# Turning a pair's attention probabilities with one wide transpose, and summing values in quarters of 32 rows

## The chip, the core and the metric

The kernel runs on one core of one Trainium2 chip. The metric is the device time of one execution in microseconds; the median of three runs of the kernel before is 863.86 (863.07 to 864.49). TensorE is called PE in the profile (PEld for its weight loads), VectorE is DVE, ScalarE ACT, GpSimd POOL, and the queue that issues most DMAs is SP.

## What is computed

Attention over 8 batches of 8 heads, 576 tokens, 64 dimensions, followed by a feed-forward layer over the joined heads:

```python
mask_local = (rel >= 0) & (rel < stride)                                  # stride 32
mask_strided = (rel >= 0) & (pos[None, :] % stride == pos[:, None] % stride)
masks = [mask_local if h < H // 2 else mask_strided for h in range(H)]
scores = where(masks, scale * (q @ k.T), -1e9)
attn = softmax(scores)                       # max subtracted, sum + 1e-9
x = (attn @ v) -> 4608 tokens x 512
h = x @ w_in                                 # 512 x 2048
g = maximum(h, 0) + log1p(exp(-abs(h)))
out = g @ w_out                              # 2048 x 512
```

## The kernel before

**Pairs of heads.** Two heads are worked on together: a pair n of 32 in all, four to a batch. The first eight (batches 1 and 2) run in an opening part whose order is written out by hand. The other 24, n = 8 to 31, are the ones that the change touches. In strided heads the tokens are sorted by their class beforehand, so that in both kinds of head a block of 32 queries sees only 64 keys: its own block and the one before it. There are 18 blocks to a head. They are held as nine blocks in each of two halves of the partitions ("place" 0 and 1), and in each half 32 partitions are for one head and 32 for the other.

**Stages of one pair.** `head_scores` (L402) makes 36 matmuls of 64 rows of weights by 32 columns, with 64 columns of keys streamed: nine blocks, two places, two heads. Six blocks of a place go to the bank ps, three to the upper part of the bank po; in those three the two heads change places in the partitions (`place_of`), and their matmuls are interleaved with the other ones. `add_mask` (L461) adds the mask on DVE in two pieces and brings the scores to SBUF. Row maximum, subtraction, exponential (ACT), row sum and normalisation follow, on tiles of 128x576. Then `prob_transposes` (L516) turns the probabilities in blocks of 32 by 32: per pair 16 DVE instructions, which write a layout of tiles with 96 queries and 128 keys. `weighted` (L584) makes 12 matmuls over it: six tiles of queries, two heads, with 128 rows, of which 32 keys overlap with the next tile, and 96 columns streamed. The first six go to the lower part of the next pair's bank po, the others to a bank ph. `x_part` copies each half to the input of the feed-forward layer, first its high part on ACT (L635), then the remainder by a subtraction on DVE (L633).

**The feed-forward layer.** It works on chunks of 512 tokens. `hidden` (L718) makes 12 matmuls into a bank ph for 128 of the 2048 hidden features; ACT (L730 to L735) and DVE (L742) make the softplus, ACT and DVE split it into a high and a low part (L287, L772), and `output` (L787) makes 12 matmuls into the four banks py. Later chunks go in pairs by products of sums (L890). There are two ph banks.

**The order.** From batch 3 on a planner (`Plan`) sets it: each task has a due time, an engine, a cost and tasks that it follows, and the tasks are issued in the order of planned starts. Between two pairs stand three steps of the feed-forward layer. On PE the scores of pair n and the weighted sums of pair n-1 form one task; with it 22 pairs' scores stand together with another pair's sums, two blocks of scores stand alone, and two blocks of sums. Behind such a block stands one `output`, then a `hidden`. For it the planner asks that the subtractions of the pair's sums be done, and its ph bank must have been read by L742.

**Loads.** `load_v` fetches a pair's values with two DMAs on SP (96 rows, then 128 rows by five tiles) into `v_in`; it is issued once the pair before has been summed. The masks come once in the beginning, as bf16, on ACT's queue.

Of the kernel before, what the change touches and what calls it, by code (L numbers as in the profile page):

```python
# [9 lines left out]
F32 = mybir.dt.float32  # L10
F32R = mybir.dt.float32r
BF16 = mybir.dt.bfloat16
# [6 lines left out]
P = 128  # L19
# [5 lines left out]
SPLIT = [(0, 6), (6, 9)]  # L25
# [51 lines left out]
class Plan:  # L77
# [8 lines left out]
    def add(self, name, urgency, engine, cost, fn, after=(), late=0.0):  # L86
        self.tasks[name] = (urgency, len(self.tasks), engine, cost, fn, after, late)
# [29 lines left out]
def attention_softplus_ffn(  # L117
# [75 lines left out]
    def x_at(part, k, c):  # L193
# [13 lines left out]
        early[part, PAIRS[-1]][:, lo : lo + 4 * TILE].rearrange("p (h a c) -> p h a c", h=2, a=2)  # L207
        for part, lo in (("l", PAD + S), ("l", PAD + S + 4 * TILE), ("h", 2 * S))
    ]
    qT = homes[0][:, 2 * S : 3 * S]  # L210
    kT = [homes[2][:, i * (PAD + S) : (i + 1) * (PAD + S)] for i in range(2)]
    v_in = homes[1][:, 2 * S : 2 * S + 2 * NTILE * D]
    prob_all = homes[1][:, : 2 * S]
    prob = [t.rearrange("p (a c) -> p a c", c=64) for t in (prob_all[:, :S], prob_all[:, S:])]

# [39 lines left out]
    def k_of(n):  # L255
        return kT_early[n] if n < NPAIR else kT[n % 2]
# [11 lines left out]
    def prob_of(n):  # L268
        if n < NPAIR:
            chunks = prob_early[n][:, PAD:].rearrange("p (a c) -> p a c", c=3 * PAD)  # L270
            return chunks[:, :, :64]
        return prob[n % 2]
# [37 lines left out]

    def load_v(n):
        b, pair = order[n]
        if n < NPAIR:

            t = room[n]
        else:
            t = v_in
        t = t[:, : 2 * NTILE * D].rearrange("p (a c) -> p a c", c=2 * D)
        src = v[b, pair]
        nc.sync.dma_start(t[PAD:P, 0], src[0:TILE])  # L320
        src = src[TILE - PAD : 2 * TILE]
        src = bass.AP(
            tensor=src.tensor,
            offset=src.offset,
            ap=[src.ap[0], [TILE * 2 * D, NTILE - 1], src.ap[1]],
        )
        nc.sync.dma_start(t[:, 1:NTILE], src)
        vs[n] = t.rearrange("p a (h d) -> p a h d", d=D)
# [12 lines left out]
    def mask_of(n, part):  # L341

        if is_local(n):
            return mask_b[:, : 6 * 64] if part == 0 else mask_b[:, 64 : 4 * 64]
        if part == 0:
            return mask_b[:, 6 * 64 : 9 * 64].unsqueeze(1).broadcast_to([P, 2, 3 * 64])
        return mask_b[:, 9 * 64 :]
# [38 lines left out]
    def head_scores(n):  # L386

        taken.append(n)
        pss[n, 0] = ps_s.tile([P, 512], F32, tag="ps", name=f"ps_{n}")
        shared[n] = ps_o.tile([P, 512], F32, tag="po", name=f"po_{n}")  # L390
        pss[n, 1] = shared[n][:, S // 2 :]
        for x in range(6):
            for chunk in (x, x + 3) if x > 2 else (x,):
                part = chunk // 6
                for place in range(2):
                    a, i = block_at(chunk, place)
                    c = TILE * a + 32 * i
                    for h in range(2):
                        to = 64 * place + 32 * place_of(part, h)
                        head = slice(64 * h, 64 * h + 64)  # L400
                        at = 64 * (chunk - SPLIT[part][0])
                        nc.tensor.matmul(  # L402
                            pss[n, part][to : to + 32, at : at + 64],
                            lhsT=qT[head, c : c + 32],
                            rhs=k_of(n)[head, c : c + 64],
                            start=True,
                            stop=True,
                        )
# [98 lines left out]
    def prob_transposes(n, quarters=range(4)):  # L507
        p = prob_of(n)
        for quarter in quarters:
            for place, h in (divmod(quarter, 2),):  # L510
                for part, (lo, hi) in enumerate(SPLIT):
                    row = 64 * place + 32 * place_of(part, h)
                    src = p[row : row + 32]
                    a, i = block_at(lo, place)
                    for c in range(2):
                        nc.vector.transpose(  # L516
                            pt[
                                32 * (i + c) : 32 * (i + c) + 32,
                                h,
                                a : a + hi - lo,  # L520
                                32 * i : 32 * i + 32,
                            ],
                            src[:, lo:hi, 32 * c : 32 * c + 32],
                        )

    def early_transposes(n, g):
# [602 lines left out]
    plan = Plan()  # L1129
    add = plan.add  # L1130

    def lows_of(c):
        return [
            f"L{n}{half}"
            for n in range(2 * NPAIR, len(order))
            if START[c] < (order[n][0] + 1) * S and START[c] + CH[c] > order[n][0] * S
            for half in range(2)
        ]
# [49 lines left out]
            add(f"G{c}.{f}", when[old] + 2.5, "SP", 0.8, fn, after, 3.5)  # L1188

    def sums_of(n):  # L1190
        for half in range(2):
            weighted(n, half, n not in alone)

    def scores_of(n, x, y, name, e, cost, after, also=None):

        z = x - 11.0
        if n > 2 * NPAIR:
            add(f"Q{n}", z, "ACT", 1.4, lambda n=n: lay_out_q(n), [f"q{n}", f"S{n-1}"])

        def work():  # L1200
            head_scores(n)
            if also is not None:
                sums_of(also)

        add(name, x, e, cost, work, after)
        for j in range(2):
            fn = lambda j=j: add_mask(n, j)
            add(f"Y{n}{j}", y + j, "DVE", 0.47, fn, [f"S{n}", f"P{n-2}"])
        after = [f"Y{n}0", f"Y{n}1"]
        for j, (letter, e, cost, fn) in enumerate(  # L1210
            (
                ("x", "DVE", 0.75, row_maxima),
                ("s", "DVE", 0.75, row_subtract),
                ("E", "ACT", 0.7, row_exp),
                ("z", "DVE", 0.75, row_sums),
                ("g", "DVE", 0.16, lambda n: guard(n, nc.vector)),
                ("R", "DVE", 0.2, reciprocals),
                ("M", "DVE", 0.75, lambda n: normalize(n, nc.vector)),
            )
        ):  # L1220
            add(f"{letter}{n}", y + 1.5 + j, e, cost, lambda fn=fn: fn(n), after)
            after = [f"{letter}{n}"]
        for j in range(4):
            name = f"P{n}" if j == 3 else f"P{n}.{j}"
            fn = lambda j=j: prob_transposes(n, (j,))
            add(name, y + 8.5 + 1.3 * j, "DVE", 1.25, fn, after)
            after = [name]
        if n + 2 < len(order):
            add(f"k{n+2}", x + 5, "SP", 0.8, lambda: load_k(n + 2), [f"S{n}"], 2.0)
            add(f"q{n+2}", x + 18, "SP", 0.8, lambda: load_q(n + 2), [f"P{n}"], 2.0)  # L1230
# [432 lines left out]
```

## Time and profile before

| | us |
|---|---|
| median of three runs | 863.86 |
| the profiled execution | 865.16 |
| its span, first to last instruction | 863.1 |
| DVE busy on L516, 448 transposes | 140.7 |
| sum of the records of PE multiplies on L402, by bank (2016 records) | 27.8 and 22.0 |
| ACT busy in all | 492.2 |

A row of the page's fifth part names line, engine, operation, tiles and shape, then the summed time and the mean of one instruction. PE's records overlap, so their summed times are not the time that PE spends: that is read from when the next block starts. In the instructions in order of time, neighbours with the same line and tiles are merged, with their count at the end. The idle time in brackets is that of the engine before the row, with what ended it.

### The profile page before, as it was taken

Reading aid. Unit: us, or ns where it says so; the run is one execution under the profiler, and the core shown is the slowest. Engines: PE = TensorE matmul, PEld = TensorE weight load, DVE = VectorE, ACT = ScalarE, POOL = GpSimd, SP = SyncE. Lnnn points to the kernel's source line nnn. Section 1 sums busy time; section 2 is a strip of 40 time slices with the busy share of each in tenths; the row PEclk is TensorE's granted clock in tenths of the full one; section 3 lists DMA queues with packets and bytes.
Section 4 is the critical chain, followed back from the end, with each engine's and each line's share of the span. In section 5 each row is a group of like instructions: output and inputs, shape, how many; then the busy total and the mean of one; then the engine's idle time right before and its main releaser. Section 6 shows DMA issues by size and latency. Waiting matters only on the chain.

```text
span 863.1 us, 16559 instructions
## 1 busy us (share of the span) xinstructions
PE 853.4 (99%) x6536; PEld 700.7 (81%) x6536; DVE 640.9 (74%) x1370; ACT 492.2 (57%) x913; POOL 65.9 (8%) x88
## 2 busy tenths in 40 slices
PE   7999999999999999999999999999999999999998
PEld 6787888888888888888888888888888888888886
DVE  7899977898798879888788976677687746656500
ACT  6898755655555555546555555766664355566400
POOL 6345550000000000000000000000000000000000
PEclk9999999999999999999999999999999999999999
DMA  9794114646313453135424433655546143333100
GB/s 330 284 348 155 55 42 152 205 148 218 119 46 99 132 185 106 58 107 164 126 86 145 142 106 118 202 176 169 175 147 197 50 158 134 111 124 120 47 27 24
DMA packets 74477, 119.49 MB, mean 138 GB/s; under 512 B 5664, under 2 KB 41632, under 8 KB 74400
## 3 DMA queue, kind: packets, MB, share of 16 engines
q1 hardware_dynamic: 74112, 118.12, 41.4%
q8 instruction: 51, 0.84, 0.4%
q10 hardware_dynamic: 288, 0.33, 0.1%
q14 instruction: 26, 0.21, 0.1%
HBM read 88.01 MB, written 30.41 MB: 137 GB/s over the span
## 4 chain that ended last, share of the span: by engine, by line
PE 92%; DVE 4%; ACT 2%; issue 1%; DMA 0%; POOL 0%; ACTq 0%; POOLq 0%
PE py L787 43%; PE ph L718 23%; PE bank_a L890 10%; PE bank_c L890 5%; PE bank_b L890 2%; PE pv L584 2%; PE ps L402 2%; PE po L584 2%; PE py_last L787 1%; PE po L402 1%; PE pt L554 1%; DVE home L516 1%; DVE a_i L672 0%; DVE a_o L672 0%; DMA raw_q<-in_qk_dram 0%
## 5 line engine op out<-in xcount | busy, mean ns | idle before, releaser
L787 PE MATMUL py<-w_o,gh 128*128 128x512 f32 x1024 | 318.5, 392 | 0.0
L787 PEld LDWEIGHTS py<-w_o,gh 128*128 128x128 f32 x1024 | 190.3, 188 | 41.4 <-DVE o L287 0.3
L718 PE MATMUL ph<-x_h,w_i 128*128 128x512 f32 x656 | 202.8, 390 | 0.5 <-DVE u L742 0.5
L787 PE MATMUL py<-w_o,gl 128*128 128x512 f32 x512 | 199.3, 389 | 0.0
L516 DVE STREAM_TRANSPOSE home<-home 32x192 f32<-32x192 f32 x448 | 140.7, 318 | 7.1
L718 PEld LDWEIGHTS ph<-x_h,w_i 128*128 128x128 f32 x656 | 122.6, 188 | 26.7 <-POOL home L505 0.9
L718 PE MATMUL ph<-x_l,w_i 128*128 128x512 f32 x328 | 127.7, 389 | 0.0
L287 ACT CAST gh<-u 128x512 fp32r<-128x512 f32 x89 | 55.2, 621 | 107.7 <-DVE u L742 84.7
L787 PEld LDWEIGHTS py<-w_o,gl 128*128 128x128 f32 x512 | 96.1, 188 | 20.3
L730 ACT ACTIVATE u<-ph 128x512 f32<-128x512 f32 x84 | 50.1, 598 | 90.8 <-PE ph L718 88.2
L772 DVE TENSOR_TENSOR gl<-u,gh 128x512 fp32r<-128x512 f32 x117 | 80.8, 691 | 19.3 <-ACT gh L287 15.7
L735 ACT ACTIVATE u<-u 128x512 f32<-128x512 f32 x144 | 90.9, 632 | 3.8
L733 ACT ACTIVATE u<-u 128x512 f32<-128x512 f32 x144 | 90.9, 632 | 3.6
L718 PEld LDWEIGHTS ph<-x_l,w_i 128*128 128x128 f32 x328 | 61.6, 188 | 13.0
L742 DVE SCALAR_TENSOR_TENSOR u<-ph,u 128x512 f32<-128x512 f32 x84 | 57.7, 687 | 13.7 <-ACT u L735 12.5
L730 ACT ACTIVATE u<-kept 128x512 f32<-128x512 f32 x45 | 28.4, 631 | 41.1 <-DVE kept L986 25.6
L287 DVE COPY o<-py 128x512 f32<-128x512 f32 (+1 forms) x15 | 10.0, 669 | 45.6 <-PE py L787 45.5
L986 DVE TENSOR_TENSOR kept<-bank_c,kept 128x512 f32<-128x512 f32 x15 | 10.4, 692 | 33.8 <-PE bank_c L890 33.8
L287 ACT COPY home<-home 128x576 f32<-128x576 f32 x26 | 33.4, 1284 | 1.7 <-DMA home<-in_qk_dram 1.7
L287 ACT COPY o<-py 128x512 f32<-128x512 f32 (+1 forms) x21 | 11.5, 574 | 38.4 <-PE py L787 27.6
L461 DVE TENSOR_TENSOR home<-ps,home 128x384 f32<-128x384 f32 x28 | 15.5, 554 | 23.5 <-PE ps L402 22.0
L981 ACT COPY kept<-bank_a 128x512 f32<-128x512 f32 x30 | 17.6, 586 | 25.8 <-PE bank_a L890 24.2
(197 smaller groups left out, 1188.7 us busy)
## 6 DMA issues: line engine op xcount, KB each, us to landing
home<-in_qk_dram SPq DMA_DIRECT2D x56, 288.0 KB, 3.2
ws<-far SPq DMA_DIRECT2D x30, 512.0 KB, 3.3
home<-in_v_dram SPq DMA_DIRECT2D x28, 320.0 KB, 3.8
out_dram<-o SPq DMA_DIRECT2D x35, 256.0 KB, 2.4
ri<-in_moe_w_in_dram SPq DMA_DIRECT2D x16, 512.0 KB, 7.4
ro<-in_moe_w_out_dram SPq DMA_DIRECT2D x16, 512.0 KB, 8.3
far_w<-w_i SPq DMA_DIRECT2D x16, 512.0 KB, 4.7
w_i<-far_w SPq DMA_DIRECT2D x16, 512.0 KB, 3.3
```

What stands on the lines that cost most here:

```text
L287: (engine.copy if engine is nc.scalar else engine.tensor_copy)(dst, src)
L402: nc.tensor.matmul(pss[n, part][to : to + 32, at : at + 64], lhsT=qT[head, c : c + 32], rhs=k_of(n)[head, c : c + 64], start=True, stop=True,)
L516: nc.vector.transpose(pt[32 * (i + c) : 32 * (i + c) + 32, h, a : a + hi - lo, 32 * i : 32 * i + 32,], src[:, lo:hi, 32 * c : 32 * c + 32],)
L584: nc.tensor.matmul(po[64 * h : 64 * h + 64, TILE * x : TILE * x + TILE], lhsT=vs[n][:, a, h, :], rhs=pt_of(n, a)[:, h, a % 2], start=True, ...
L718: nc.tensor.matmul(ph, lhsT=w_i(c, f)[:, half, cc * P : (cc + 1) * P], rhs=x_at(x, cc, c), start=(i == 0), stop=(i == 3 * NCC - 1),)
L730: nc.scalar.activation(us[c, f], phs[c, f], AF.Abs)
L733: nc.scalar.activation(u, u, AF.Exp, scale=-1.0)
L735: nc.scalar.activation(u, u, AF.Ln, bias=1.0)
L742: nc.vector.scalar_tensor_tensor(to, in0=ph, scalar=0.0, in1=u, op0=ALU.max, op1=ALU.add)
L772: engine.tensor_tensor(g, us.pop((c, f)), ghs[c, f].bitcast(F32), op=ALU.subtract)
L787: nc.tensor.matmul(y_of(c, t), lhsT=g[:, sl], rhs=w32["o", f][:, half], start=(f == ROWS[c][0] and n == 0), stop=(f == ROWS[c][-1] and n = ...
L890: nc.tensor.matmul(bank, lhsT=w_left(p, A, f, half, i), rhs=x_right(p, A, part, i), start=p in "125" and n == 0, stop=n == 5, skip_group_c ...
```

## The change

For pairs 8 to 31, and for these alone:

- Scores: the nine blocks of a place are now nine neighbouring blocks of the sequence, in order, and the heads keep their 32 partitions in all of them. The count and the shapes of the matmuls stay.
- One transpose of 128x576 (`turn`) takes the place of the 16. It writes `turned`: for each quarter of 32 partitions (place and head) and each block, 32 keys by 32 queries, twice (the block before and the own one).
- `turned_sums` takes the place of `weighted`: for each of nine blocks, two key blocks, two places and two heads a matmul with 32 rows of values (64 columns of weights) and 32 queries streamed, two of them accumulated: 72 matmuls instead of 12. Place 0 goes to the bank that took the first half before, place 1 to that of the second, and the two are filled side by side.
- `load_v` fetches the values so that each quarter has its head's blocks of 32 keys: four DMAs in pieces of 64 elements instead of two.
- A mask in the new order of blocks is loaded once more for the strided heads, in six DMAs.
- In the planner the four tasks of the transposes become one with a cost of 0.8.

```diff
+    turned = homes[0][:, :S].rearrange("p (x c l) -> p x c l", c=2, l=32)
+    v_turned = homes[1][:, 2 * S : 2 * S + (NCHK + 1) * D]
+    mask_turned = homes[0][:, 3 * S : 3 * S + NCHK * 32].bitcast(BF16)
...
     def load_v(n):
         b, pair = order[n]
+        if n >= 2 * NPAIR:
+            t = vs[n] = v_turned.rearrange("p (x d) -> p x d", d=D)
+            if n == 2 * NPAIR:
+                nc.gpsimd.memset(t[:64, 0], 0.0)
+            for place in range(2):
+                blocks = slice(32 * (NCHK * place - place), 32 * NCHK * (place + 1))
+                src = v[b, pair][blocks].rearrange("(x k) (h d) -> h k x d", k=32, h=2)
+                for h in range(2):
+                    at = 64 * place + 32 * h
+                    nc.sync.dma_start(t[at : at + 32, 1 - place :], src[h])
+            return
...
     def head_scores(n):
...
+        if n >= 2 * NPAIR:
+            for chunk in range(NCHK):
+                part = chunk // 6
+                at = 64 * (chunk - SPLIT[part][0])
+                for place in range(2):
+                    c = 32 * (NCHK * place + chunk)
+                    for h in range(2):
+                        to = 64 * place + 32 * h
+                        head = slice(64 * h, 64 * h + 64)
+                        nc.tensor.matmul(
+                            pss[n, part][to : to + 32, at : at + 64],
+                            lhsT=qT[head, c : c + 32],
+                            rhs=k_of(n)[head, c : c + 64],
...
+            return
...
+    def turn(n):
+        src = prob_of(n).rearrange("p x (c l) -> p x c l", l=32)
+        nc.vector.transpose(
+            turned.rearrange("p x c l -> p (x c) l"), src.rearrange("p x c l -> p (x c) l")
+        )
+
+    def turned_sums(n, joint):
...
+        pos[n, 0], pos[n, 1] = banks_
+        for x in range(NCHK):
+            for c in range(2):
+                for place in range(2):
+                    for h in range(2):
+                        at = 64 * place + 32 * h
+                        rows = slice(at, at + 32)
+                        nc.tensor.matmul(
+                            banks_[place][64 * h : 64 * h + 64, 32 * x : 32 * x + 32],
+                            lhsT=vs[n][rows, x + c],
+                            rhs=turned[rows, x, c],
+                            start=c == 0,
+                            stop=c == 1,
                         )
...
     def sums_of(n):
-        for half in range(2):
-            weighted(n, half, n not in alone)
+        turned_sums(n, n not in alone)
...
-        for j in range(4):
-            name = f"P{n}" if j == 3 else f"P{n}.{j}"
-            fn = lambda j=j: prob_transposes(n, (j,))
-            add(name, y + 8.5 + 1.3 * j, "DVE", 1.25, fn, after)
-            after = [name]
+        add(f"P{n}", y + 8.5, "DVE", 0.8, lambda: turn(n), after)
```

On PE, the block of a pair's scores and of the sums of the pair before, in the middle of the program, before (ps and po take the scores, po and pv the sums, home_94 to home_96 are the SBUF rooms of queries and probabilities, of values, and of keys):

```order
L718 MATMUL ph_13_3614<-x_l_594,w_i_13_3558 128x512
L402 MATMUL ps_3638<-home_96,home_94 32x64 x16
L402 MATMUL po_3639<-home_96,home_94 32x64 x4
L402 MATMUL ps_3638<-home_96,home_94 32x64 x4
L402 MATMUL po_3639<-home_96,home_94 32x64 x4
L402 MATMUL ps_3638<-home_96,home_94 32x64 x4
L402 MATMUL po_3639<-home_96,home_94 32x64 x4
L584 MATMUL po_3639<-home_94,home_95 64x96 x6
L584 MATMUL pv_3682<-home_94,home_95 64x96 x6
L787 MATMUL py_106<-w_o_1590,gh_11_3585 128x512 x2
```

and the same block with the change, where the two rows of sums repeat 18 times:

```order
L417 MATMUL ps_4017<-home_96,home_94 32x64 x24
L417 MATMUL po_4018<-home_96,home_94 32x64 x12
L583 MATMUL po_4018<-home_94,home_95 64x32 x2
L583 MATMUL pv_1_4055<-home_94,home_95 64x32 x2
L583 MATMUL po_4018<-home_94,home_95 64x32 x2
```

The two banks of scores no longer alternate, and those of sums do; apart from these blocks PE's order is the same in both programs.

On DVE behind such a block, before (L461 adds the mask, L633 makes the low part of the sums, L742 the softplus, L516 turns):

```order
L461 TENSOR_TENSOR home_95<-ps_3638,home_97 128x384 [waits DMAHW0_49,PE_49]
L461 TENSOR_TENSOR home_95<-po_3639,home_97 128x192 [waits PE_49,Activation_49]
L633 TENSOR_TENSOR x_l_406<-po_3639,x_h_364 128x256
L633 TENSOR_TENSOR x_far_3714<-po_3639,x_far_3714 128x32
L466 TENSOR_REDUCE st_3716<-home_95 128x9 [waits DVE_49]
L633 TENSOR_TENSOR x_far_3714<-pv_3682,x_far_3714 128x288 [waits Activation_49]
L742 SCALAR_TENSOR_TENSOR u_13_3689<-ph_13_3614,u_13_3689 128x512
...
L505 TENSOR_TENSOR home_95<-home_95,st_3716 128x576 [waits DVE_49]
L516 STREAM_TRANSPOSE home_94<-home_95 32x6x32 [waits DVE_49]
L516 STREAM_TRANSPOSE home_94<-home_95 32x6x32
L516 STREAM_TRANSPOSE home_94<-home_95 32x3x32 x2
```

and with the change:

```order
L494 TENSOR_TENSOR home_95<-ps_4017,home_94 128x384 [waits DMAHW6_49,PE_49]
L494 TENSOR_TENSOR home_95<-po_4018,home_94 128x192 [waits PE_49,Activation_49]
L698 TENSOR_TENSOR x_l_406<-po_4018,x_h_364 128x256
L698 TENSOR_TENSOR x_far_4147<-po_4018,x_far_4147 128x32
L499 TENSOR_REDUCE st_4149<-home_95 128x9 [waits DVE_49]
L698 TENSOR_TENSOR x_far_4147<-pv_1_4055,x_far_4147 128x288 [waits Activation_49]
L807 SCALAR_TENSOR_TENSOR u_13_4128<-ph_13_4000,u_13_4128 128x512
...
L538 TENSOR_TENSOR home_95<-home_95,st_4149 128x576 [waits DVE_49]
L562 STREAM_TRANSPOSE home_94<-home_95 128x576 [waits DVE_49]
L807 SCALAR_TENSOR_TENSOR u_14_4197<-ph_14_4164,u_14_4197 128x512 [waits Activation_49]
```

The lines are numbered anew, and the order up to the softplus stands as before, with the second mask piece still waiting for ACT; the transposes are one instruction.

More of the change, by code (lines that the diff above doesn't have):

```diff
@@ L344, in mask_of @@
             return mask_b[:, : 6 * 64] if part == 0 else mask_b[:, 64 : 4 * 64]
+        if n >= 2 * NPAIR:
+            return mask_turned[:, : 6 * 64] if part == 0 else mask_turned[:, 6 * 64 :]
         if part == 0:
@@ L391, in head_scores @@
         pss[n, 1] = shared[n][:, S // 2 :]
+        if n >= 2 * NPAIR:
+            for chunk in range(NCHK):
[10 more added lines that the diff above has]
+                            rhs=k_of(n)[head, c : c + 64],
+                            start=True,
+                            stop=True,
+                        )
+            return
         for x in range(6):
@@ L523, in prob_transposes @@
                             src[:, lo:hi, 32 * c : 32 * c + 32],
+                        )
+    def turn(n):
+        src = prob_of(n).rearrange("p x (c l) -> p x c l", l=32)
+        nc.vector.transpose(
+            turned.rearrange("p x c l -> p (x c) l"), src.rearrange("p x c l -> p (x c) l")
+        )
+    def turned_sums(n, joint):
+        if joint:
+            banks_ = [shared[n + 1], ps_h.tile([P, 512], F32, tag="ph", name=f"pv_{n}_1")]
+        else:
+            taken.append(n)
+            banks_ = [
+                ps_o.tile([P, 512], F32, tag="po", name=f"pv_{n}_0"),
+                ps_s.tile([P, 512], F32, tag="ps", name=f"pv_{n}_1"),
+            ]
+        pos[n, 0], pos[n, 1] = banks_
[11 more added lines that the diff above has]
+                            stop=c == 1,
                         )
@@ L1130, in attention_softplus_ffn, with load_mask @@
     add = plan.add
+    def load_mask():
+        for place in range(2):
+            to = mask_turned[64 * place : 64 * place + 64].rearrange("p (a x c) -> p x a c", x=3, c=64)
+            for x, (half, at) in enumerate(((0, 6), (place, 9), (1, 6))):
+                src = masks[64 * half : 64 * half + 64, 64 * at : 64 * at + 3 * 64]
+                nc.sync.dma_start(to[:, x], src.rearrange("p (a c) -> p a c", c=64))
+    add("mask", 0.0, "SP", 1.5, load_mask, [], 2.0)
     def lows_of(c):
```

## Prediction

> **What bounds the kernel now.** I read the page's busy rows first, then the table of stages, then the instructions in order of time around one pair of heads.
>
> ```profile
> span 863.1 us, 16559 instructions
> PE 853.4 (99%) x6536; PEld 700.7 (81%) x6536; DVE 640.9 (74%) x1370; ACT 492.2 (57%) x913; POOL 65.9 (8%) x88
> PE 92%; DVE 4%; ACT 2%; issue 1%; DMA 0%; POOL 0%; ACTq 0%; POOLq 0%
> 134.00:500.00 366.00, 366.00 (x3309) 300.96 (x3302) 309.63 (x721) 207.02 (x358) 0.00 (x0) 1.00 0.41 132
> 548.00:700.00 152.00, 152.00 (x1001) 125.35 (x988) 108.98 (x217) 84.40 (x144) 0.00 (x0) 1.00 0.48 151
> ```
>
> The last two rows are stages in microseconds, with the busy time of PE, PEld, DVE, ACT and POOL. They hold nearly all the work that changes, and in both PE has no idle time at a granted clock of 1.00. DVE has 56 us spare in the first and 43 us in the second. So the time moves by what PE's instructions cost, and by any wait put in front of them; work taken from DVE buys nothing there. This is one pair's block on PE, with what ACT and DVE do behind it:
>
> ```profile
> 188.39 0.39 PE L718 MATMUL ph<-x_l,w_i 128*128 128x512 f32 x1
> 188.71 0.48 PE L402 MATMUL ps<-home,home 64*32 64x64 f32 x20
> 188.98 0.24 PE L402 MATMUL po<-home,home 64*32 64x64 f32 x1
> 189.01 0.24 PE L402 MATMUL ps<-home,home 64*32 64x64 f32 x4
> 189.04 0.26 PE L402 MATMUL po<-home,home 64*32 64x64 f32 x3
> ...
> 189.50 0.27 PE L402 MATMUL po<-home,home 64*32 64x64 f32 x4
> 189.70 0.72 PE L584 MATMUL po<-home,home 128*64 128x96 f32 x12
> 190.24 0.67 PE L584 MATMUL pv<-home,home 128*64 128x96 f32 x12
> 190.64 0.38 ACT L635 CAST x_h<-po 128x288 fp32r<-128x288 f32 x1
> 190.84 0.73 PE L787 MATMUL py<-w_o,gh 128*128 128x512 f32 x2
> ...
> 191.06 0.36 DVE L461 TENSOR_TENSOR home<-po,home 128x192 f32<-128x192 f32 x1 [0.76 <-ACT x_h L635]
> ...
> 192.78 0.68 DVE L742 SCALAR_TENSOR_TENSOR u<-ph,u 128x512 f32<-128x512 f32 x1
> ...
> 193.69 0.62 PE L718 MATMUL ph<-x_h,w_i 128*128 128x512 f32 x2
> ```
>
> Columns: start, length, engine, line, operation, output and inputs, rows*columns of the weights, shape, count. An f32 matmul leaves two records, so 36 score matmuls (L402) are 72 records and 12 weighted sums (L584) are 24. Scores take 189.70 - 188.71 = 0.99 us from first start to the next block's; the sums take 190.84 - 189.70 = **1.14 us**. Sums run at two records per 82 ns (the last of 24 starts at 190.24 + 0.67 - 0.25 = 190.66, and the first round takes some 50 ns more); the switch to the next block takes 190.84 - 190.66 = 0.18 us.
>
> **The change, part by part.** *Weighted sums.* Twelve matmuls of 128 rows by 96 columns become 72 of 32 rows by 32 columns: 144 records for 24, in four quarters of the array, 36 each. No such record is in the trace, so I bound a round, that is one record in each quarter. The multiply alone: the scores' 64 columns take 56 ns a round (next fence), 96 columns take 82, so 32 take about 30. But every record first loads its own 64 columns of weights:
>
> ```profile
> L402 PEld LDWEIGHTS ps<-home,home x1344: 102/107/108, 33.0 to 644.0; 64*32 64x32 f32 x192
> L584 PEld LDWEIGHTS pv<-home,home x372: 132/137/138, 60.8 to 671.0; 128*64 128x64 f32 x186
> L787 PEld LDWEIGHTS py<-w_o,gh 128*128 128x128 f32 x1024 | 190.3, 188 | 41.4 <-DVE o L287 0.3
> 11.96 0.91 PE L372 MATMUL py<-early_l,early_h 128*64 128x64 f32 x24
> 188.70:188.78 0.08, 0.07 (x4) 0.07 (x8) 1.00 1.09 435
> 188.70:188.84 0.14, 0.13 (x8) 0.13 (x12) 1.00 1.00 402
> ```
>
> Loads of 32, 64 and 128 columns have medians of 107, 137 and 188 ns: some 0.8 to 0.9 ns a column, so 64 columns hold a quarter for 51 to 60 ns. The early scores (L372) load 64 columns and multiply 64: the last of 24 starts at 11.96 + 0.91 - 0.22 = 12.65, so two records in two halves take 0.69 / 23 * 2 = 60 ns. The stage rows on L402 (multiplies and loads that fall into the stretch from 188.70) show 4 multiplies and 8 loads, then 8 and 12: one load ahead of each multiply, no more. So a quarter cannot go faster than its loads, and I take **59 ns** a round. 36 rounds: 35 * 0.059 + 0.05 for the first + 0.02 between the quarters + 0.18 switch = **2.31 us, +1.17 a pair**; by the multiply alone 35 * 0.030 + 0.25 = 1.30 us, +0.16.
>
> This needs four quarters at once, of which two lie one above the other in the same columns. The mixed part of the scores speaks for it: 25 records start from 188.71 to 189.03, before that part, at 56 ns for four, while the 47 after it take until 189.55, 11 ns each. Four places at 56 ns would give 14, so places one above the other do work at once there. If they took turns, V would have 72 rounds: 71 * 0.059 + 0.25 = 4.44 us, +3.30 a pair.
>
> The Trainium skill's page "TensorE: Matmul & The Clock Gate", section "LDWEIGHTS (loading the stationary operand)", says that a load's time goes by columns over 1.2 ns and not by rows. By that rule, 64 columns are 53 ns whether 128 or 32 rows deep, an estimate that would make the sums 35 * 0.053 + 0.25 = 2.11 us. It speaks against this change, and the rows above agree with it for columns; that 32 rows load no faster, no run here shows yet.
>
> *Scores.* The same 36 matmuls, but all nine blocks on the same four places, where before the last three blocks of a half used the other four. 72 records in 18 rounds of four at 56 ns, the first 80 (the 4 multiplies of the fence stand alone until 188.78): 0.08 + 16 * 0.056 + 0.02 = 1.00 to the last start, then the same 189.70 - 189.55 = 0.15 to the switch: 1.15 against 0.99, **+0.16 a pair**. Ends: 0 if the mixing bought nothing, +0.2.
>
> *A wait behind the sums.* In the block above, ACT's copy x_h<-po starts at 190.64, as ACT comes free, since the first half of the sums is done early. L461 on DVE waits for that copy, and behind it on DVE stand the x_l subtractions, the row maximum and L742, which frees the bank that PE's next L718 writes: 192.78 + 0.68 = 193.46 against 193.69. That is 0.23 us of slack; of the 19 such blocks from 151 to 490 us the tightest has 175.02 - 174.91 = 0.11:
>
> ```profile
> 174.23 0.68 DVE L742 SCALAR_TENSOR_TENSOR u<-ph,u 128x512 f32<-128x512 f32 x1
> 175.02 0.61 PE L718 MATMUL ph<-x_h,w_i 128*128 128x512 f32 x2
> ```
>
> After the change both halves end together. What a copy then waits is seen where sums stand alone:
>
> ```profile
> 506.33 1.21 PE L584 MATMUL pv<-home,home 128*64 128x96 f32 x24
> 507.09 0.96 ACT L635 CAST x_h<-pv 128x64 fp32r<-128x64 f32 x4 [2.47 <-PE pv L584]
> ```
>
> The twelfth of 24 records starts at about 506.33 + 0.13 + 4 * 0.082 = 506.80, and ACT follows 0.29 us later. With the first half's last record some 0.02 us before the block's last, and 0.18 from there to the switch, the copy starts 0.1 us after the next PE block instead of 0.2 before it. So L742 ends 0.3 later against PE: past 0.11 to 0.23 of slack, and with a few hundredths for the signal that makes about 0.17 us of PE waiting, 19 times: **3.2 us** (0 to 6).
>
> *DVE.* Sixteen transposes go, one of 128x576 comes:
>
> ```profile
> L516 DVE STREAM_TRANSPOSE home<-home 32x192 f32<-32x192 f32 x224 | 81.8, 365 | 3.3
> L516 DVE STREAM_TRANSPOSE home<-home 32x96 f32<-32x96 f32 x224 | 60.5, 270 | 3.8
> ```
>
> Eight of each form are 5.1 us a pair; by the slope of 1 ns an element the new one takes 0.75 us (between 0.37 and 2.2, six of the long form). Some 4.3 us a pair, 104 in all, leave DVE, hidden behind PE before and after: the probabilities are wanted 18.7 us after their scores. I count 0; without cover it would be a gain of that size, but PE's 366.00 of 366.00 leaves none.
>
> *Loads.* V comes in four DMAs of 72 to 80 KB in pieces of 256 B instead of two; the mask takes six small ones once.
>
> ```profile
> home<-in_v_dram SPq DMA_DIRECT2D x28, 320.0 KB, 3.8
> q8 instruction: 51, 0.84, 0.4%
> ```
>
> The large one landed 3.8 us after issue; were it doubled, it would still be in place 10 us before the next pair's sums. SP issues two more per pair at about 0.4 us, and its queue waits on nothing nearer. I take 0; a late load would cost PE its whole lateness.
>
> *Sum.* 24 pairs: 24 * 1.17 = 28.1, 24 * 0.16 = 3.8, waits 3.2: **+35.1 us** on the profiled execution's 865.2 (863.1 span and 2 around it). The median of the runs shown is 863.86, so I predict **899.0**.
>
> **The rivals.** *The columns take turns*: two quarters one above the other load in turn; 24 * 3.30 + 3.8 + 3.2 = +86, **950 us**. Against it: the 11 ns records; for it, that no 64-column load shares columns there. Chance 0.10.
>
> *The multiply alone sets the round*: a load of 32 rows is quick or hidden deeper; 24 * 0.16 + 3.8 + 3.2 = +10.8, **875 us**. Against it: one load ahead, and the early scores' 60 ns. Chance 0.11. The Trainium skill's page "TensorE: Matmul & The Clock Gate", section "Part 3: Packing small matmuls — row/col tiling", has a span model by which four small matmuls take little more than one, 4 ns a tile. By it a round would be 30 + 12 ns, an estimate near this case; no row here has four such quarters.
>
> *Instructions come too slowly*: 216 records, each with a load, make 432 instructions in 3.4 us. The page's q8 row is 16 KB a packet; 0.84 MB for 2 * 6536 PE instructions is 64 B each, so a block wants 1.7 packets, and 0.4% of 16 * 863 us over 51 packets is 1.08 us each. They should be in time; if every block waits for one, 24 * 1.08 = +26, **925 us**. Chance 0.06.
>
> *On the other side*: the small pieces all start as fast as PE starts anything. In this stretch the first four multiplies lie within 0.03 us:
>
> ```profile
> 188.70:188.73 0.03, 0.02 (x4) 0.02 (x4) 1.00 0.74 290
> ```
>
> At some 7 ns a record through both blocks, loads hidden behind other places, a pair takes 216 * 0.007 + 0.18 = 1.7 us against 2.13: -10 us and waits of 3, **857 us**. It decides below 9 ns a record. Against it: after those four none starts for 50 ns. Chance 0.05, of which 0.02 falls within 0.2%.
>
> **How the numbers follow.** My forecast has 0.68. With the 875 case, and what lies between, the range from 872 to 915 holds about 0.8; it leaves out 950, 925 and the fast side. 0.2% is about what a measurement of this kernel can tell from no change: faster 0.03, same 0.02, slower 0.95.
>
> **What would show it.** Per pair, sums of 2.3 us in 36 rounds of 59 ns (30 means the multiply, 118 turns); scores of 1.15; L718 after a pair waiting 0.1 to 0.3 us on L742; DVE busy down by 100 us with no gain; PE otherwise without idle time. If sums are 2.3 us but the time does not rise by 28, PE's time was not the bound.

## The result, and the profile after

| | us | to before |
|---|---|---|
| before, median of 3 runs | 863.86 | |
| after, median of 4 runs (925.39 to 927.08) | 926.31 | 1.0723 (1.0704 to 1.0742) |
| predicted | 899.0 (872 to 915) | |
| profiled execution, before and after | 865.16 and 927.08 | +61.9 |

The change makes the kernel slower by 7%, 62 us where 35 were forecast, and outside the range. The page of after begins, as that of before did, with the span, the busy time of each engine and, from its fourth part, the chain that ended last; the last row counts the packets of 16 KB that bring instructions.

```profile
span 925.3 us, 22062 instructions
...
PE 897.9 (97%) x9416; PEld 742.0 (80%) x9416; DVE 539.3 (58%) x1010; ACT 494.1 (53%) x913; POOL 66.1 (7%) x89
...
q8 instruction: 74, 1.21, 0.5%
...
PE 91%; issue 3%; DMA 2%; DVE 2%; ACT 1%; POOL 0%; SPq 0%; ACTq 0%; POOLq 0%
```

DVE gave up 101.6 us (640.9 to 539.3) and nothing came of it. PE went from 99% busy to 97%, and "issue", time in which it waited for nothing that the profile shows, from 1% to 3% of the chain. The waits of PE (total, times, longest) say where. First before, then after:

```profile
PE pt L554 <- issue: 2.8, 2, 1.6
...
PE py L372 <- issue: 0.5, 2, 0.3
```

```profile
PE pv L583 <- issue: 9.6, 6, 2.5
PE po L583 <- issue: 7.0, 5, 2.6
PE pt L619 <- issue: 2.5, 2, 1.5
```

The new weighted sums (L583) have eleven waits without a releaser, up to 2.6 us long. Now two blocks of scores and sums in the table of stages, with the busy time and count of PE, PEld, DVE, ACT and POOL, then the granted clock, and at the end the DMA's busy share and its GB/s. The first two rows are one block's scores and its sums, the other rows the sums of another block and what comes behind.

```profile
195.59:196.73 1.14, 1.14 (x74) 1.05 (x73) 0.20 (x1) 1.00 (x2) 0.00 (x0) 1.00 0.65 243
196.73:198.96 2.23, 2.23 (x151) 2.19 (x145) 0.36 (x1) 0.85 (x2) 0.00 (x0) 1.00 0.46 122
...
152.16:153.88 1.72, 1.72 (x123) 1.72 (x117) 0.36 (x1) 0.86 (x2) 0.00 (x0) 1.00 0.86 246
153.90:155.93 2.03, 0.20 (x13) 0.08 (x5) 0.00 (x0) 0.00 (x0) 0.00 (x0) 1.00 0.33 119
155.94:156.52 0.58, 0.58 (x27) 0.54 (x27) 0.00 (x0) 0.00 (x0) 0.00 (x0) 1.00 0.00 0
156.72:160.13 3.41, 3.41 (x9) 2.66 (x9) 3.11 (x8) 2.42 (x6) 0.00 (x0) 0.50 0.60 167
160.13:163.54 3.41, 3.41 (x17) 2.81 (x16) 3.23 (x6) 0.66 (x1) 0.00 (x0) 1.00 0.21 83
```

The first block takes 1.14 + 2.23 us. In the other the sums start at 152.16 and run as fast, stop at 153.88 with some 27 records to go, and go on at 155.94; nothing at all starts on PE for 2.06 us. Then, from 156.72, the granted clock is 0.50 for 3.41 us, and PE does 9 multiplies where the next 3.41 us hold 17. In the instructions in order of time the standstill is one row with a wait that nothing releases:

```profile
153.87 0.23 PE L583 MATMUL po<-home,home 32*64 32x32 f32 x2
155.94 0.24 PE L583 MATMUL pv<-home,home 32*64 32x32 f32 x2 [1.84 <-issue]
...
156.52 0.64 PE L852 MATMUL py<-w_o,gh 128*128 128x512 f32 x1
```

Of the 24 blocks of sums 12 take 2.23 us and 12 take 2.62 to 5.55; together these are 20.3 us over 12 * 2.23. The granted clock is halved for seven times 3.41 us, in six places, each beginning no more than 1.6 us after such a standstill ends: 23.9 us, of which half is lost. So the profiled execution's +61.9 us comes apart:

| | us |
|---|---|
| scores, 24 * (1.14 - 0.99) | 3.6 |
| sums without standstill, 24 * (2.23 - 1.14) | 26.2 |
| standstills in 12 blocks of sums | 20.3 |
| half clock, 23.9 / 2 | 11.9 |
| sum | 62.0 |

Two more standstills, 0.7 and 1.2 us, lie just behind a block, and part of the half clock falls into other waits, so the sum is good to some 2 us. The first two terms are those that the prediction forecast; the last two, 32 us, are like the rival to which it gave 0.06.

### The profile page after: what moved, and what is told of

Same layout as the page of the kernel before. It is cut to its first block, busy times and chain, and to the rows that moved or that the text cites. A ratio compares the mean times of both kernels' runs of the same rounds, so it can differ in the third digit from the quotient of the medians.

```text
span 925.3 us, 22062 instructions
## 1 busy us (share of the span) xinstructions
PE 897.9 (97%) x9416; PEld 742.0 (80%) x9416; DVE 539.3 (58%) x1010; ACT 494.1 (53%) x913; POOL 66.1 (7%) x89
## 4 chain that ended last, share of the span: by engine, by line
PE 91%; issue 3%; DMA 2%; DVE 2%; ACT 1%; POOL 0%; SPq 0%; ACTq 0%; POOLq 0%
PE py L852 41%; PE ph L783 22%; PE bank_a L955 9%; PE bank_c L955 4%; PE po L583 4%; PE bank_b L955 2%; PE pv L583 2%; PE ps L417 2%; DMA ro<-in_moe_w_out_dram 2%; PE py_last L852 1%; PE po L417 1%; PE pv L649 1%; PE pt L619 1%; DVE home L549 0%; DMA raw_q<-in_qk_dram 0%
## 5 line engine op out<-in xcount | busy, mean ns | idle before, releaser
L852 PE MATMUL py<-w_o,gh 128*128 128x512 f32 x1024 | 324.3, 398 | 0.0
L852 PEld LDWEIGHTS py<-w_o,gh 128*128 128x128 f32 x1024 | 194.2, 191 | 40.9
L783 PE MATMUL ph<-x_h,w_i 128*128 128x512 f32 x656 | 203.0, 391 | 0.5 <-DVE u L807 0.5
L852 PE MATMUL py<-w_o,gl 128*128 128x512 f32 x512 | 202.6, 396 | 0.5 <-issue 0.5
L783 PEld LDWEIGHTS ph<-x_h,w_i 128*128 128x128 f32 x656 | 122.8, 188 | 27.1 <-POOL home L538 0.9
L783 PE MATMUL ph<-x_l,w_i 128*128 128x512 f32 x328 | 127.7, 389 | 0.0
L852 PEld LDWEIGHTS py<-w_o,gl 128*128 128x128 f32 x512 | 98.0, 191 | 22.0 <-issue 0.9
L807 DVE SCALAR_TENSOR_TENSOR u<-ph,u 128x512 f32<-128x512 f32 x84 | 57.6, 686 | 82.3 <-ACT u L800 82.2
L783 PEld LDWEIGHTS ph<-x_l,w_i 128*128 128x128 f32 x328 | 61.6, 188 | 13.1
L583 PE MATMUL pv<-home,home 32*64 32x32 f32 x1872 | 57.9, 219 | 9.7 <-issue 9.6
L583 PEld LDWEIGHTS pv<-home,home 32*64 32x64 f32 x1872 | 53.9, 133 | 13.9 <-issue 13.5
L583 PE MATMUL po<-home,home 32*64 32x32 f32 x1584 | 52.8, 219 | 7.0 <-issue 7.0
L583 PEld LDWEIGHTS po<-home,home 32*64 32x64 f32 x1584 | 49.2, 133 | 6.8 <-issue 4.8
L494 DVE TENSOR_TENSOR home<-po,home 128x192 f32<-128x192 f32 x28 | 9.9, 355 | 68.4 <-ACT x_h L700 54.1
```

The lines of the kernel that those rows point to most:

```text
L494: nc.vector.tensor_tensor(pv, sv, m, op=ALU.add)
L583: nc.tensor.matmul(banks_[place][64 * h : 64 * h + 64, 32 * x : 32 * x + 32], lhsT=vs[n][rows, x + c], rhs=turned[rows, x, c], start=c == ...
L783: nc.tensor.matmul(ph, lhsT=w_i(c, f)[:, half, cc * P : (cc + 1) * P], rhs=x_at(x, cc, c), start=(i == 0), stop=(i == 3 * NCC - 1),)
L807: nc.vector.scalar_tensor_tensor(to, in0=ph, scalar=0.0, in1=u, op0=ALU.max, op1=ALU.add)
L852: nc.tensor.matmul(y_of(c, t), lhsT=g[:, sl], rhs=w32["o", f][:, half], start=(f == ROWS[c][0] and n == 0), stop=(f == ROWS[c][-1] and n = ...
```

## The experiments

**Theory A**: PE stands still because its instructions are not there yet. **Theory B** is the rival that each expectation names: the small transfers, the data or the contents of the block. Times are medians, with their range, the count of runs and the ratio to before.

**1. Scores alone.** The kernel before, with the two heads kept in their partitions, which puts the nine blocks on four places.

```diff
     def place_of(part, h):
-        return 1 - h if part == 1 else h
+        return h
```

> The kernel before, but the heads keep their partitions in all nine blocks, so the 36 matmuls of scores use four places instead of eight; nothing else changes, and it holds for 28 pairs. If places one above the other work at once, 0.15 us more a pair: 28 * 0.15 = 4.2, 868.1. If the mixing bought nothing: 863.9.

868.3 (867.94 to 868.83, 5 runs), 1.0054 (1.0040 to 1.0068). Scores take 1.14 us in every block, and the edit holds for the 28 pairs whose scores L402 makes, four of them in the opening: 28 * 0.15 = 4.2 of the 4.4 measured. The change itself touches 24 of them, which makes the 3.6 above.

**2. The transpose alone.** The kernel before, with one transpose of 128x576 for the 16; the sums then read a layout that is not theirs.

```diff
-        for j in range(4):
...
+        def turn():
+            src = prob_of(n).rearrange("p x (c l) -> p (x c) l", l=32)
+            to = homes[0][:, :S].rearrange("p (x l) -> p x l", l=32)
+            nc.vector.transpose(to, src)
...
+        add(f"P{n}", y + 8.5, "DVE", 0.8, turn, after)
```

> The kernel before, but with one transpose of 128x576 from n = 8 on instead of 16 (the sums of these pairs then read a layout that isn't theirs). Some 100 us less work on DVE. If PE is the bound throughout: 863.9 within 0.5. If DVE's work holds PE up somewhere: 858 to 862.

863.41 (862.55 to 864.75, 10 runs), 0.9995 (0.9986 to 1.0004): no change. The DVE time that the change frees is worth nothing.

**3. Long pieces for V.** The change, with V loaded in pieces of 2.3 KB and more instead of 256 B; the sums then meet other keys than their own.

```diff
-                src = v[b, pair][blocks].rearrange("(x k) (h d) -> h k x d", k=32, h=2)
+                src = v[b, pair].rearrange("(k y) c -> k (y c)", k=32)
...
-                    nc.sync.dma_start(t[at : at + 32, 1 - place :], src[h])
+                    lo, wide = 1152 * h, D * (NCHK + place)
+                    to = v_turned[at : at + 32, D * (1 - place) :]
+                    nc.sync.dma_start(to, src[:, lo : lo + wide])
```

> The changed kernel, but the values are loaded in contiguous pieces of 2.3 KB and more instead of 256 B (they land in another order, so the sums are over the wrong keys; every instruction on the engines stays). Theory A (PE runs out of fetched instructions because a block has 432 of them): no change, 926 us within 4. Theory B (the small pieces of the values' loads hold up the instruction fetches): the standstills inside the sums go, 20 us, and the half clock after them, 12 us: about 895.

921.75 (920.98 to 923.93, 4 runs), 1.0669 (1.0651 to 1.0687). The same 12 blocks stand still, 18.95 us in sum, with 23.9 us of half clock: it is not the transfers. The time is 4.6 us below that of after, just outside the expected 4; the standstills account for 20.3 - 18.95 = 1.4 of it. The small pieces may cost the rest; which wait that would be is not shown.

**4. Many instructions in the old kernel.** The kernel before with every score matmul of the planned pairs made three times: 480 PE instructions in a block, and neither the new sums nor the new loads.

```diff
-        for x in range(6):
+        for x in [*range(6)] * (3 if n >= 2 * NPAIR else 1):
```

> The kernel before, but each pair from n = 8 on makes its scores three times over (the same matmuls, written again): 480 PE instructions in a block of one pair, with loads and sums as before. Unhindered the two extra rounds take some 0.9 us each, 24 * 1.8 = 43, so 907. Theory A: standstills of PE within the block as in the changed kernel, 20 us or more, and half clock after some of them: 925 to 960. Theory B: none of it, 905 to 910.

959.84 (956.03 to 963.64, 2 runs), 1.1113 (1.1062 to 1.1164). The waits of PE in this kernel:

```profile
PE ps L402 <- issue: 27.5, 13, 3.6
PE po L402 <- issue: 4.9, 3, 2.7
PE pv L584 <- issue: 4.9, 2, 4.0
```

Old matmuls over old data stand still as the new ones do. Theory B in these forms falls, and theory A stands. 17 of 24 blocks of scores are disturbed, and 5 of sums, two of these by the half clock alone.

**5. Scores and sums apart.** The change, with the sums a step of the feed-forward layer (5.7 us) behind the scores in all but the last joint blocks: 144 and 288 instructions instead of 432 at once.

```diff
+        scores_of(n, x, x + 1.5, f"S{n}", "PE", cost, after)
         if joint(i):
...
-        scores_of(n, x, x + 1.5, f"S{n}", "PE", cost, after, n - 1 if joint(i) else None)
+            free = [f"S{n}", f"P{n-1}", f"v{n-1}", f"u{i}"]
+            add(f"V{n-1}", when[i + 1], "PE", 2.5, lambda n=n: sums_of(n - 1), free)
...
```

> The changed kernel, but a pair's sums stand one step of the feed-forward layer (about 5.7 us) behind the next pair's scores, in 19 of the 22 joint blocks. Loads, matmuls and DVE work are the same. The switch of shape comes once more, 0.32 us each, 6 us in all. Theory A: blocks of 288 and of 144 instructions instead of 432, so standstills and half clock mostly go: 864 + 3.6 scores + 26 sums + 6 = 900, up to 906. Theory B: the loads are as small as before, so they stay: 926 + 6 = 932.

904.16 (902.29 to 905.40, 4 runs), 1.0466 (1.0450 to 1.0483). Every block of sums takes 2.23 us but one (5.13), a block still joint; 6.8 us of half clock. The work is the same and 22 us are gone.

**6. Half of the sums.** The change without the block of keys before: 36 matmuls instead of 72, 288 instructions in a block.

```diff
-            for c in range(2):
+            for c in (1,):
...
-                            start=c == 0,
+                            start=True,
```

> The changed kernel, but only the own block of keys is summed (36 matmuls for 72; the block before is left out). 18 rounds of 59 ns and 0.25 make 1.25 us against 1.14, +3 us, and the scores' 3.6: 870 without standstills. Theory A: 288 instructions a block, few standstills: 870 to 878. Theory B: all loads are still there: 890 to 902.

867.72 (867.36 to 867.78, 3 runs), 1.0044 (1.0028 to 1.0060), 2.3 us below the expected range: sums take 1.18 us and no block stands still at all, with the clock at 1.00 throughout.

**7. Twice the multiply.** The change with 64 columns streamed instead of 32 (every sum but the last of a row also computes the columns of its neighbour).

```diff
-                            banks_[place][64 * h : 64 * h + 64, 32 * x : 32 * x + 32],
+                            banks_[place][64 * h : 64 * h + 64, 32 * x : 32 * x + 64 - 32 * (x == 8)],
...
-                            rhs=turned[rows, x, c],
+                            rhs=turned[rows, x, c] if x == 8 else wide_of(rows, x, c),
```

> The changed kernel, but each sum streams 64 columns instead of 32 (the upper 32 are overwritten by the next block's), with the same weight loads and the same count of instructions. If the load of 64 columns sets a round, a block of sums without a standstill stays at 2.23 us, and the time near 926 (918 to 930). If the multiply set it, 30 more ns in 36 rounds make it 3.3 us and the time 940 or more.

917.8 (917.11 to 918.49, 2 runs), 1.0625 (1.0605 to 1.0644). That is 0.2 below the expected range. Undisturbed sums still take 2.23 us: the columns that are streamed do not set the round. Standstills are 19.2 us in 11 of the same 12 blocks; that it is 8 us faster than after comes from the clock, halved for 10.2 us instead of 23.9.

**8 to 10. The same program, shifted.** In experiments 3 and 7, whose PE instructions are as many as those of after, the same blocks stood still. So the place in the stream of instructions may decide. Three runs repeat 32, 16 and 48 matmuls in the last pair of the opening part, far ahead, which adds 128, 64 and 192 instructions.

```diff
-        for x in range(6):
+        for x in [*range(6)] + ([0, 1, 3, 4, 5] if n == 2 * NPAIR - 1 else []):
```

> The change, with 32 matmuls of the last pair of the opening part made twice: 64 more records and as many loads on PE, some 0.9 us, long before the first block of the change. Counting two instructions a record from the start, the blocks of scores and sums of the change begin, within the 256 instructions of a 16 KB packet, at 44, 108, 172 and 236, the same four places in each batch; sums had a standstill in 6 of 6 blocks (with the last, at 0) that begin at 44 or 0, 3 of 5 at 108, none of 5 at 172, 3 of 5 at 236. The 128 added instructions turn 44 into 172 and 108 into 236. Theory A (PE waits for instructions, in packets): blocks 1, 5, 9, 13 and 17, all disturbed in the change, have sums of 2.23 us here, and blocks 3, 7, 11, 15 and 19, all at 2.23 in the change, take 3 to 5.5 us; the time stays within 915 to 935 us. Theory B (what a block does, its heads, its data or its transfers make the standstill): the same blocks 1, 2, 5, 6, 8, 9, 10, 12, 13, 16, 17, 21 are disturbed as in the change, and the time is 927 us.

930.1 (927.61 to 930.57, 4 runs), 1.0769 (1.0751 to 1.0787). Blocks 1, 5, 9, 13 and 17 all take 2.23 us now, and 3, 7, 11, 15 and 19, undisturbed in after, take 3.57, 3.08, 3.46, 5.00 and 5.20.

> The same with 16 matmuls made twice, 64 instructions: the blocks that began at 44, 108, 172 and 236 begin at 108, 172, 236 and 44. Theory A: blocks 2, 6, 10, 14 and 18 have sums of 2.23 us, blocks 4, 8, 12, 16 and 20 are all disturbed, by 1 to 3.3 us; 915 to 935 us. Theory B: the same blocks as in the change.

931.3 (929.12 to 933.78, 4 runs), 1.0782 (1.0754 to 1.0809). Blocks 2, 6, 10, 14 and 18 take 2.23; 4, 8, 12 and 16 take 3.16, 4.66, 3.62 and 3.17, but 20 does not: it is one of the two in which sums stand alone, with 288 instructions.

With these runs the place could be counted exactly. The table of stages counts PE's multiplies and loads from the start to where PE goes on, for after and, in the opening, for before:

```profile
0.00:155.93 155.93, 148.53 (x1619) 120.86 (x1619) 130.38 (x277) 113.00 (x259) 66.06 (x89) 1.00 0.59 203
```

```profile
0.00:16.56 16.56, 12.70 (x221) 8.61 (x222) 12.68 (x32) 9.52 (x19) 11.31 (x37) 1.00 0.94 316
0.00:22.76 22.76, 17.26 (x349) 12.99 (x350) 17.07 (x42) 13.73 (x33) 14.04 (x40) 1.00 0.97 329
```

To these come the semaphore instructions of PE's sequencer, which the trace holds but no view counts: 27 by then in after, 6 in before. 1619 + 1619 + 27 = 3265 = 12 * 256 + 193; 221 + 222 + 6 = 449 = 256 + 193; 349 + 350 + 6 = 705 = 2 * 256 + 193. All 13 standstills of over 0.8 us that after has in its sums and in the opening's transposes, and all 15, 15 and 13 of the shifted kernels, end at instruction 193 of a group of 256, one packet. (That it is 193 depends on where the count begins, here with the first instruction of PE in the trace.) And a block stands still only where this instruction lies deep in it. The last shift was made to try that rule ahead of the run.

> The change, with 48 matmuls of the last pair of the opening part made twice: 96 more records and as many loads on PE, about 1.4 us, before the first block of the change. In the runs so far every standstill ends with the 193rd of 256 PE instructions, counted over multiplies, loads and the sequencer's semaphore instructions, and it comes only where that instruction is more than about 296 instructions into a block of scores and sums. Theory A (the store of instructions is empty there; the next packet is asked for some 300 instructions ahead): shifted by 192 instructions, the blocks that have such an instruction at 304 to 428 stand still, which are 2, 3, 6, 7, 9, 10, 13, 14, 17, 18 and 23 of 24; block 11, with it at 295, is on the edge (0 to 0.4 us); all others, 1, 4, 5, 8, 12, 15, 16, 19 to 22 and 24, have sums of 2.23 us. The time is 924 to 936 us. Theory B (the standstills only scatter around the places found, and the count of instructions is a coincidence): other blocks too, or some of these without one.

925.62 (923.63 to 928.47, 4 runs), 1.0719 (1.0691 to 1.0747). Disturbed are exactly the eleven named, by 0.95 to 4.60 us; block 11 and all others take 2.23. Over the four kernels, by where instruction 193 stands in a block (counted from the block's first; 24 blocks with sums each):

| kernel | at 300 or more: blocks, disturbed | at 294 to 297 | nowhere past 293: blocks, disturbed |
|---|---|---|---|
| after | 11, 11 | one at 297: 2.62 us | 12, 0 |
| shifted by 64 | 13, 13 | none | 11, 0 |
| shifted by 128 | 13, 13 | one at 294: 2.23 us | 10, 0 |
| shifted by 192 | 11, 11 | one at 295: 2.23 us | 12, 0 |

The one disturbed block of experiment 5 has it at 371; in experiment 6, with 288 instructions, it is nowhere past 288. Theory A is settled, with the place. That the place is near 300 goes with the pace of these blocks: in experiment 4, where 432 instructions take 2.55 us undisturbed against 3.37 here, two blocks with instruction 193 at 287 and 289 also took 0.6 and 0.5 us longer.

**11 and 12. One load for two blocks of queries.** The change with 40 matmuls instead of 72: a block of keys is loaded once and multiplied with the queries of both blocks that see it. 304 instructions in a joint block. First with the odd blocks of keys first, where later starts wipe out part of the sums begun before; then in order, each bank cleared by its first matmul alone.

```diff
-        for x in range(NCHK):
-            for c in range(2):
+        for j in range(NCHK + 1):
+            lo, hi = max(j - 1, 0), min(j, NCHK - 1)
...
-                            lhsT=vs[n][rows, x + c],
-                            rhs=turned[rows, x, c],
-                            start=c == 0,
+                        lhsT=vs[n][rows, j],
+                        rhs=homes[0][rows, first : first + 32 * (hi - lo + 1)],
+                        start=j == 0,
```

> The changed kernel with the sums regrouped: one weight load of a key block serves both blocks of queries that see it, 40 matmuls with 64 columns for 72 with 32. 20 rounds at the load's 59 ns and 0.25 make 1.43 us, 24 * 0.29 = 7.0 over before, and 3.6 for the scores; 304 instructions a block, as many as ran without a standstill: 874.5. If the standstills came from the changed loads or the mixed banks rather than the count: 890 or more. If multiplies of 64 columns in four quarters take turns: 885 or more.

874.71 (874.52 to 877.82, 4 runs), 1.0134 (1.0118 to 1.0151): sums of 1.32 us, one block with a standstill (3.95).

> The change with one weight load for each block of 32 keys, used for the two blocks of queries that see it at once: 40 matmuls of 32 rows by 64 queries for the sums instead of 72 of 32, in the order of the keys, each bank cleared by its first matmul alone. 304 PE instructions in a joint block instead of 432, as in the run with the odd key blocks first. Theory A: sums of 1.32 us as there, 24 * (1.32 - 1.14) = 4.3 and 3.6 for the scores, and not more than two standstills with their half clock, 0 to 7 us: 872 to 879 us, likeliest 875. Theory B (a standstill is chance): the same mean, but up to 885. If the clearing costs or the order makes a quarter wait for itself, sums of 1.5 us and more, 879 us or more.

873.85 (873.62 to 876.17, 4 runs), 1.0122 (1.0107 to 1.0137): sums of 1.30, one block at 2.52, the clock at 1.00. The disturbed block, the eighth in both, has instruction 193 at its 303rd. This is the fastest form of the change that was run and that makes all the sums, and it is still 10 us behind the kernel before, whose sums take 1.14 and whose scores take 0.99.

## Why the prediction was right and wrong

**What bounds the kernel** was right: some 102 us less work on DVE (104 were forecast) were worth nothing (experiment 2 alone, 863.41), and time moved by what PE did.

**Sums without standstill**: forecast 2.31 us in rounds of 59 ns set by the load, +28.1 us; measured 2.23, +26.2. The rounds start 58 ns apart (198.50, 198.56, 198.61 and so on to 198.79 for the bank po). Experiment 7 rules out the multiply. That it is the load, and not a cost that each record has whatever its columns, fits the loads of 64 columns that the forecast rested on, but no run changed the columns loaded while 32 were streamed, so it is not shown. Two quarters one above the other do work at once: 144 records in 36 rounds are what 2.23 us hold, and by turns they would have taken 4.44.

**Scores**: forecast +0.16 a pair, measured +0.15 (experiment 1).

**The wait behind the sums**: forecast 3.2 us, measured none. The copies did come later, as worked out, but the step that L742 (now L807) frees the bank of the next L718 (L783) was wrong. After:

```profile
198.96 0.73 PE L852 MATMUL py<-w_o,gh 128*128 128x512 f32 x2
...
201.25 0.68 DVE L807 SCALAR_TENSOR_TENSOR u<-ph,u 128x512 f32<-128x512 f32 x1
...
201.81 0.62 PE L783 MATMUL ph<-x_h,w_i 128*128 128x512 f32 x2
```

The softplus runs until 201.93, and the hidden step starts at 201.81, ahead of its end: it does not wait for it. From this block to the next undisturbed one are 215.51 - 195.59 = 19.92 us, 1.24 more than the 18.68 of before, which is 0.15 + 1.09 and leaves nothing for a wait; from the first `output` after the block to the hidden step it is 201.81 - 198.96 = 2.85 us, as before (193.69 - 190.84).

**The loads**: forecast 0, at most 4.6 us by experiment 3.

**The step that failed** is in the rivals: "They should be in time". It held 1.7 packets of 1.08 us a block against 3.4 us, an average and the length of a packet. But what counts is how far ahead the next packet is asked for and how long until its instructions can be used. The trace holds the start of every packet: none starts before PE stands near instruction 150 of a group, PE never gets past instruction 193 of the group behind without it, and it goes on 2.2 to 3.0 us after the packet's start (up to 3.8 us in other runs, where the packet itself took about 2 us). For the standstill shown above, the view of the DMA queues from 153.69, where the packet starts, to 155.94 has the row `q8 instruction: 1, 0.02, 2.6%`, and from 136.70 to 153.69 it has none of q8. Some 297 instructions are thus all that it has in hand. At the pace of a block, 432 in 3.37 - 0.18 us, they last 2.2 us; in the feed-forward layer, with about 20 of them in 2.2 us, they last more than ten times as long. A block of 432 instructions can hold the whole stretch from the request to the end of the store, and then it runs dry; the 192 of before never could.

The rival's price, one packet's length in every block, was also wrong: it is 0.4 to 3.3 us in half of them. And no rival had the clock that falls behind a standstill, 11.9 us. That its 925 lies 1 us from the measured 926.31 is luck: its 26 us for the packets stand against 20.3 for the standstills and 11.9 for the clock, and the 3.2 of the wait behind the sums and 2 of the sums' own 28.1 were not there.

The page of before could have told. The row of waits on L554 shown above, 2.8 us in two waits, was there, and in the instructions in order of time both of its standstills lie within a run of equal matmuls with nothing to wait for, and both, by the count above, at instruction 193:

```profile
14.82 0.57 PE L554 MATMUL pt<-room,early_l 128*64 128x64 f32 x13
16.57 0.27 PE L554 MATMUL pt<-room,early_l 128*64 128x64 f32 x2 [1.17 <-issue]
...
20.48 0.65 PE L554 MATMUL pt<-room,early_l 128*64 128x64 f32 x15
22.77 0.22 PE L554 MATMUL pt<-room,early_l 128*64 128x64 f32 x1 [1.64 <-issue]
```

The Trainium skill's page "Runtime: NRT & Kernel Launch", section "Instruction fetch mechanics", has the refill in blocks of 256 instructions, and says that the cost of crossing one is "mostly hidden". The traces agree on the 256 (and on one packet a group); hidden it is at the pace of the large matmuls, and not at 7 ns an instruction.

**What stays open**: what sets the moment of the request. Packets that hold up nothing also start well past instruction 150, in before up to 67 instructions into the next group; and standstills differ in length (0.4 to 4.6 us), mostly by how late their packet starts.

## What to carry to other kernels

Count the instructions of PE, and not only its columns: splitting a matmul into small ones multiplies loads and multiplies, and here a run of 432 short ones came to a stop for 0.4 to 4.6 us wherever the end of a packet fell at about its 300th or later, whatever they computed. An "issue" wait in the middle of a run of equal instructions is the sign, and spreading the run out among long matmuls (experiment 5, -22 us) or sharing a load between two multiplies (experiment 12, -52 us) is the remedy. Here 36 rounds of 58 ns took the place of 12 of 82, so that a quarter of the rows and a third of the streamed columns bought nothing.

## What was not expected of the hardware

- PE ran out of instructions at instruction 193 of each 256, in every kernel, that of before included, and went on mostly 2.2 to 3.0 us after a packet of 16 KB started, though the packet itself mostly took 0.9 to 1.6 us.
- The granted clock falls to 0.50 after some standstills, for 3.41 us at a time. A standstill of 2.06 us was enough, one of 1.35 us too (at 259.59 us of after), while 1.55 us (at 473.99) left the clock at 1.00. The half clocks begin whole multiples of 3.413 us apart (156.72 and 262.53: 31 of them), so they keep to a fixed grid of windows. PE was busy for 2.28 us of the window from 259.12, which holds the second standstill and was followed by the half clock, and for 2.07 us of that from 474.16, which holds most of the third and was not; what decides it stays open. The Trainium skill's page "TensorE: Matmul & The Clock Gate", section "Part 1: The HAM clock gate (the "warmup" mystery)", has a free-running window of 3413 ns, which fits the lengths and the grid; its condition of an idle window does not fit, since PE was idle for less than half of the 3.41 us in the second of these cases.
- 32 rows load no faster than 128. A record of a load of 64 columns takes 133 ns in the new sums (mean, below), against a median of 137 in the old ones with 128 rows.

```profile
L583 PEld LDWEIGHTS pv<-home,home 32*64 32x64 f32 x1872 | 53.9, 133 | 13.9 <-issue 13.5
```
